# Filter taps sent through DRAM instead of turned on TensorE, in a gated mix of linear attention and a long convolution on one core

## The chip, the core and the metric

The kernel runs on one core of a Trainium2 chip. Its time is the device time of one execution in microseconds; the kernel before takes 174.07 us (median of three runs, 173.83 to 174.19). Engines are named as the profile names them: PE is TensorE's matmul and PEld its weight load, DVE is VectorE, ACT is ScalarE, POOL is GpSimd, SP is SyncE, whose queue issues nearly all transfers.

## The reference, cut to what matters

A sequence `x` of S = 2048 rows with D = 448 features goes through a linear attention block and through a state-space convolution, and a gate mixes the two:

```python
g = sigmoid((x * gate_w).sum(-1, keepdims=True))
qkv = x @ wqkv                                  # 16 heads of 28
pq, pk = phi(q), phi(k)                         # phi(t) = (t + 1 if t > 0 else exp(t)) + 1e-6
kv, z = sum over s of pk[s]^T v[s], sum over s of pk[s]
a = (pq @ kv / (pq . z + 1e-6)) @ wo
dt = exp(log_dt);  A = -exp(log_A_real) + 1j*A_imag;  C = (C_real + 1j*C_imag)*dt
K[d, l] = 2 * Re(sum over n of C[d, n] * exp(A[d, n]*dt[d]*l))      # N = 256
b = causal convolution of x with K along the sequence + x * D_skip
out = g*a + (1 - g)*b
```

With these inputs the exponent is so small that, channel by channel, `K[d, l]` is the same tap for all lags; the kernel tests this and has a general path behind a branch that isn't taken. So the convolution is a running sum of `x` times one tap per channel: 448 taps.

## The kernel before, in words

The sequence is cut into NC = 16 chunks of 128 rows. The matmuls split each fp32 operand into a high part and a low part, so that one projection of a chunk is 11 products. The order of all instructions is written out by hand; each engine works off its own queue in that order, and SP's queue too.

The main loop runs over c = 2 to 13 (L476). At step c PE computes the key projection of chunk c+1 (`project` with tag "k" or "v1", L484), the query projection of chunk c (L494), 11 products into the sums `g` (`do_g(c)`, L518), and from c = 5 on two running sums of two products each (`do_v`, L408). So one step is 37 products on PE. Around it:

- `split_t(c + 2)` casts the turned chunk on ACT (L240) and makes its low part `xt` on POOL (L241, shown as L236, the helper `low`). The second product of the next step's key projection reads that low part.
- `k_feature`, `k_high`, `k_low` (L357 to L372) work on the key projection in its PSUM bank "k"; the last instruction of `k_low` frees the bank for the next step's projection.
- `q_post` (L379) does the same for the query projection.
- `split_n(c + 2)` casts the plain chunk on ACT (L246), makes the low part `xn` on POOL, and with `skip` (L252) puts `x * D_skip` into `y` on POOL.
- `v_post(c)` (L413) multiplies the running sum of a chunk, in PSUM bank "v0" or "v1" by parity, with the taps `near` on DVE (L415), sends the last row to `u` with two small transfers on SP (L418), and adds the product to `y` on POOL (`v_add`, L423).
- `load_x(c + 3)` (L478) asks for a chunk of `x`, on SP, as the first thing of the step; there are four buffers.

The taps come from `s4d_prepare` (L279), a generator that `steps` advances a bit in each of the steps c = 1 to 5. Its small sums on DVE, on 112 partitions by 4 columns, end with `p0` in step 4 (L308). Channel d = 112 j + r stands at partition r, column j. In step 5, between the query projection and `do_g(5)`, its last part (L311 to L314) turns `p0`, spread over 128 columns, with four TensorE transposes into a PSUM bank, and ACT copies the bank to `near`, the first of the two parts of `rows`: every partition then holds all 448 taps in the order of the channels.

`VS` (L35) says which running sums belong to which step: 0 and 1 to step 5, 2 and 3 to step 6, and so on; the first of a pair stands behind the key projection, the second behind the query projection. Step 5 is an exception: its sum 1 stands behind `do_g(5)`, and `v_post(0)` and `v_post(1)` stand on either side of the instructions of `split_n(7)`.

The parameters of the sums come in as `abc`, four pieces of 112 x 1024 numbers, in the place of the chunks 6 to 15 of `pq` (L205, L229). The last chunk of `pq` is written only near the end, by `late`.

Of the kernel before, what the change touches and what calls it, by code (L numbers as in the profile page):

```python
# [7 lines left out]
F32 = mybir.dt.float32  # L8
# [3 lines left out]
ALU = mybir.AluOpType  # L12
# [3 lines left out]
P = 128  # L16
S = 2048
D = 448
# [3 lines left out]
NC = S // P  # L22
J = 4
DJ = D // J
# [7 lines left out]
QA = 1  # L32
QW = 512
EDGE = 16
VS = {c: (2 * c - 10, 2 * c - 9) for c in range(5, 11)} | {c: (c + 1,) for c in range(11, NC - 1)}  # L35
SMALL = 2.0 ** -70
FLAT = 2.0 ** 35
BIG = 3.4028234e38
# [102 lines left out]
def gated_mix_kernel(ctx: ExitStack, tc: tile.TileContext, xin, wq_d, wvo_d, abc_d, ldt_d, dsk_d,  # L141
                     turn_d, cst_d, first_d, gin_d, out):
    nc = tc.nc
    PE, ACT, DVE, POOL, SP = nc.tensor, nc.scalar, nc.vector, nc.gpsimd, nc.sync

    keep = ctx.enter_context(tc.tile_pool(name="keep", bufs=1))
    pq = keep.tile([P, NC, D], F32, name="pq")
# [9 lines left out]
    work = ExitStack()  # L157
# [7 lines left out]
    ident, trir = both[:, 0], both[:, 1]  # L165
# [5 lines left out]
    near, dsk = (rows[:, i * D:(i + 1) * D] for i in range(2))  # L171
# [12 lines left out]
    xn_p = work.enter_context(tc.tile_pool(name="xn", bufs=7))  # L184
    tp = work.enter_context(tc.tile_pool(name="tp", bufs=2))
    ps = work.enter_context(tc.tile_pool(name="ps", bufs=1, space=PSUM))

    warm = tp.tile([P, 512], mybir.dt.bfloat16, name="warm", tag="e")
    POOL.memset(warm, 1.0)
# [7 lines left out]
    def load_x(c):  # L197
        r = xp.tile([P, XC], F32, name="xr", tag="xr")
        turned[c], plain[c] = r[:, :NAT], r[:, NAT:]
        SP.dma_start(out=r, in_=xin[c])  # L200
# [4 lines left out]
    abc = pf[:DJ, 3 * J * N:7 * J * N].rearrange("p (i j n) -> p i j n", i=4, j=J)  # L205
    wkr = {}
    o = 0
    for part in PARTS:
# [8 lines left out]
        o = e  # L217
# [8 lines left out]
    SP.dma_start(out=dsk, in_=dsk_d.to_broadcast([P, D]))  # L226
    load_x(3)
    SP.dma_start(out=ldt, in_=ldt_d)
    for i in range(4):  # L229
        SP.dma_start(out=abc[:, i], in_=abc_d[:, i])  # L230
        if i == 0:
            load_x(4)
    SP.dma_start(out=both, in_=turn_d)

    def low(eng, o, r, h):
# [2 lines left out]
    def split_t(c):  # L238
        w = xt[c] = xt_p.tile([P, 2 * NAT], F32R, name="xt", tag="t")
        ACT.copy(w[:, :NAT], turned[c])  # L240
        low(POOL, w[:, NAT:], turned[c], w[:, :NAT])  # L241
# [33 lines left out]
    def small():  # L275
        cnt[0] += 1
        return sm[:, cnt[0] - 1]

    def s4d_prepare():  # L279
        tt = lambda eng, o, a, b, op: eng.tensor_tensor(out=o, in0=a, in1=b, op=op)  # L280
        stt = lambda o, a, k, b, op1: DVE.scalar_tensor_tensor(out=o, in0=a, scalar=k, in1=b, op0=ALU.mult, op1=op1)
        junk = [yf[:DJ, F0 + (i - 2) * 2 * N:F0 + (i - 1) * 2 * N].rearrange("p (i n) -> p i n", i=2) for i in range(2)]
        s0, s1, dt, am, p0, p1, d2, md, b0, b1 = (small() for _ in range(10))
        for j in range(J):
            ACT.activation(abc[:, 0, j], abc[:, 0, j], AF.Exp)
        ACT.activation(dt, ldt, AF.Exp)
        tt(DVE, d2, dt, dt, ALU.mult)
        yield
        for j in range(J):
            ACT.activation(junk[0], abc[:, 0:2, j], AF.Square, accum_out=am[:, j:j + 1])  # L290
            ACT.activation(junk[0][:, 0], abc[:, 2, j], AF.Copy, accum_out=s0[:, j:j + 1])
            DVE.scalar_tensor_tensor(out=junk[1], in0=abc[:, 2:4, j], scalar=1.0, in1=abc[:, 0:2, j], op0=ALU.mult,
                                     op1=ALU.mult, accum_out=s1[:, j:j + 1])
            if j % 2:
                yield
# [12 lines left out]
        tt(DVE, p0, p0, okc, ALU.mult)  # L308
        DVE.tensor_reduce(out=oks, in_=okc, op=ALU.add, axis=AX.X)
        yield  # L310
        o = ps.tile([P, 512], F32, name="p", tag="v1")  # L311
        for j in range(J):
            PE.transpose(o[:, j * DJ:(j + 1) * DJ], p0[:, j:j + 1].to_broadcast([DJ, P]), ident[:DJ, :DJ])
        ACT.copy(near, o[:, :D])  # L314

    def pieces(c, wh, wl, n, tag, last=None):
        o = ps.tile([P, 512], F32, name=tag, tag=tag)
# [20 lines left out]
    def project(*args, **kw):  # L338
        o, run = pieces(*args, **kw)
        run(11)  # L340
        return o
# [15 lines left out]
    def k_feature(c, o):  # L357
        e = tp.tile([P, D], F32, name="e", tag="e")
        pks[c] = o[:, :D]
        ACT.activation(e, pks[c], AF.Relu, scale=-1.0)  # L360
        ACT.activation(e, e, AF.Exp, scale=-1.0)  # L361
        DVE.scalar_tensor_tensor(out=pks[c], in0=pks[c], scalar=1.0, in1=e, op0=ALU.add, op1=ALU.max)  # L362

    def k_high(c):
        pkh[c] = tp.tile([P, 512], F32R, name="pkh", tag="pkh")[:, EDGE:EDGE + D]
        ACT.add(pkh[c], pks[c], 1e-6)

    def k_low(c):
        pk = pks.pop(c)
        pkl[c] = tp.tile([P, 512], F32R, name="pkl", tag="pkl")[:, EDGE:EDGE + D]  # L370
        for o, a, op in ((pkl[c], pkh[c].bitcast(F32), ALU.subtract), (zb, zb, ALU.add))[::-1 if c == NC - 1 else 1]:
            DVE.scalar_tensor_tensor(out=o, in0=pk, scalar=1e-6, in1=a, op0=ALU.add, op1=op)  # L372
# [33 lines left out]
    vt = {}  # L406

    def do_v(c):  # L408
        v = vt[c] = ps.tile([P, 512], F32, name="v", tag="v%d" % (c % 2))
        PE.matmul(v[:, :D], lhsT=tri, rhs=xn[c][:, :D], start=True, stop=False)  # L410
        PE.matmul(v[:, :D], lhsT=tri, rhs=xn[c][:, XC - NAT:], start=False, stop=True)

    def v_post(c):  # L413
        t = tp.tile([P, D], F32, name="t", tag="v0")
        DVE.tensor_tensor(out=t, in0=vt.pop(c)[:, :D], in1=near, op=ALU.mult)  # L415
        if c < NC - 1:
            for k in (c, UL + c):
                SP.dma_start(out=u[k:k + 1], in_=t[P - 1:P])  # L418
            v_add(c, t)
        return t  # L420

    def v_add(c, t):
        POOL.tensor_tensor(out=y[:, c], in0=y[:, c], in1=t, op=ALU.add)  # L423

    prep = s4d_prepare()
# [48 lines left out]
    split_n(3)  # L474
    woh, wol = [], []
    for c in range(2, NC - 2):  # L476
        if c + 3 < NC:
            load_x(c + 3)  # L478
        if c == 2:
            SP.dma_start(out=cst, in_=cst_d)  # L480
        if c == 4:
            SP.dma_start(out=wvo, in_=wvo_d)
        vs = VS.get(c, ())
        ko = project(c + 1, wkh, wkl, D, "v1" if c in (2, 4) else "k")  # L484
        for v in vs[:1]:
            do_v(v)
        split_t(c + 2)
        k_feature(c + 1, ko)
        k_high(c + 1)
        if c > 5:  # L490
            for v in vs[:1]:
                v_post(v)
        k_low(c + 1)
        qo = project(c, wqh, wql, D + 2, "q")  # L494
        if c == 5:
            steps(1)
        else:
            for v in vs[1:]:
                do_v(v)
        q_post(c, qo)  # L500
        if c == 10:
            split_n(c + 2)
        if c == 5:
            v_post(0)
        else:
            for v in vs[1:]:
                v_post(v)
        if c < 5:
            steps(2 if c == 4 else 1)
        if c == 3:  # L510
            DVE.tensor_copy(tri, trir)
            DVE.tensor_copy(gcr, gcat)
        if c == 7:
            SP.dma_start(out=okr[:, None, :DJ], in_=oks[:, None, :])
        if c == 9:
            DVE.tensor_reduce(out=okr[:, DJ:], in_=okr[:, :DJ], op=ALU.add, axis=AX.X)
            DVE.tensor_copy(okn, okr[:, DJ:])
        do_g(c)  # L518
        if c == 5:
            do_v(1)  # L520
        if c < 4:
            skip(c - 1)
        if c != 10:
            split_n(c + 2)
        if c == 5:
            v_post(1)
        for j in {11: (0, 1), 12: (2, 3)}.get(c, ()):
            w = xn_p.tile([P, NX], F32R, name="wo", tag="n")[:DJ, :2 * D].rearrange("p (i d) -> p i d", i=2)
            woh.append(w[:, 0])
            wol.append(w[:, 1])  # L530
            ACT.copy(woh[j], wo[:, j])
            low(POOL, wol[j], wo[:, j], woh[j])
# [109 lines left out]
    c = NC - 2  # L642
# [294 lines left out]
```

## Time and profile before

| | |
|---|---|
| time, median of 3 runs | 174.07 us (173.83 to 174.19) |
| the profiled execution | 174.06 us, its span 172.2 us |
| PE busy | 167.8 us in 876 products |
| PEld, DVE, ACT, POOL busy | 152.0, 113.9, 96.0, 120.0 us |
| granted TensorE clock | 1.00 throughout |
| moved by DMA | 18.60 MB, mean 108 GB/s |

A row of the timeline gives the start and the duration in us, the engine and line, the operation, what it writes and reads, the shape, how often it stands there in a row, and in brackets the idle time of the engine before it and what ended that. SPq rows are the issue of a transfer, not the transfer. A row of a group gives the count, the busy time in us, the mean in ns, and the idle time before. Times are from the span's start. The profile's line numbers are those of the kernel before.

### The profile page before, as it was taken

Reading aid. Unit: us, or ns where it says so; the run is one execution under the profiler, and the core shown is the slowest. Engines: PE = TensorE matmul, PEld = TensorE weight load, DVE = VectorE, ACT = ScalarE, POOL = GpSimd, SP = SyncE. Lnnn points to the kernel's source line nnn. Section 1 sums busy time; section 2 is a strip of 40 time slices with the busy share of each in tenths; the row PEclk is TensorE's granted clock in tenths of the full one; section 3 lists DMA queues with packets and bytes.
Section 4 is the critical chain, followed back from the end, with each engine's and each line's share of the span. In section 5 each row is a group of like instructions: output and inputs, shape, how many; then the busy total and the mean of one; then the engine's idle time right before and its main releaser. Section 6 shows DMA issues by size and latency. Waiting matters only on the chain. (4 is left out here: it accounts for less than half of the span.)

```text
span 172.2 us, 2796 instructions
## 1 busy us (share of the span) xinstructions
PE 167.8 (97%) x876; PEld 152.0 (88%) x876; DVE 113.9 (66%) x240; ACT 96.0 (56%) x221; POOL 120.0 (70%) x128
## 2 busy tenths in 40 slices
PE   6999999999999999999999999999999999999992
PEld 2788999999899999999999999999899999999992
DVE  0847737698975483846627346487898998987542
ACT  3688588894256262542727456356574564664541
POOL 6082667877529988696996999529968998892200
PEclk9999999999999999999999999999999999999999
DMA  5989975097003031230404200000031222122213
GB/s 173 415 297 294 268 209 166 0 368 303 4 0 114 11 123 34 95 123 1 122 15 131 106 1 1 0 0 2 7 67 54 107 89 76 62 99 107 108 59 108
DMA packets 7962, 18.60 MB, mean 108 GB/s; under 512 B 2045, under 2 KB 4810, under 8 KB 7818
## 3 DMA queue, kind: packets, MB, share of 16 engines
q1 hardware_dynamic: 7802, 18.30, 32.0%
q8 instruction: 7, 0.11, 0.3%
q10 hardware_dynamic: 144, 0.11, 0.2%
q14 instruction: 9, 0.07, 0.1%
HBM read 14.38 MB, written 3.67 MB: 105 GB/s over the span
## 5 line engine op out<-in xcount | busy, mean ns | idle before, releaser
L629 PE MATMUL a<-wk,th 128*128 128x448 f32 (+1 forms) x170 | 36.4, 360 | 0.0
L403 PE MATMUL g<-pkh,xn 128*128 128x448 f32 x112 | 35.6, 364 | 0.0
L629 PEld LDWEIGHTS a<-wk,th 128*128 128x128 f32 x170 | 29.5, 189 | 1.6
L334 PE MATMUL k<-wk,xt 128*128 128x448 f32 x132 | 29.3, 367 | 0.0
L334 PE MATMUL q<-wqh,xt 128*128 128x450 f32 x120 | 27.5, 366 | 0.0
L362 DVE SCALAR_TENSOR_TENSOR k<-k,e 128x448 f32<-128x448 f32 x12 | 7.6, 632 | 29.4 <-ACT e L361 29.4
L423 POOL TENSOR_TENSOR y<-y,t 128x448 f32<-128x448 f32 x16 | 18.7, 1168 | 11.5 <-DVE t L415 11.5
L334 PEld LDWEIGHTS k<-wk,xt 128*128 128x128 f32 x132 | 24.8, 189 | 2.2 <-DVE wk L236 0.3
L334 PEld LDWEIGHTS q<-wqh,xt 128*128 128x128 f32 x120 | 22.5, 188 | 1.7
L236 POOL TENSOR_TENSOR xn<-xr,xn 128x448 fp32r<-128x448 f32 x16 | 19.4, 1211 | 6.6 <-ACT xn L246 4.5
L403 PE MATMUL g<-pkl,xn 128*128 128x448 f32 x64 | 23.4, 366 | 0.0
L403 PEld LDWEIGHTS g<-pkh,xn 128*128 128x128 f32 x112 | 21.0, 188 | 2.2
L236 POOL TENSOR_TENSOR xt<-xr,xt 128x512 fp32r<-128x512 f32 x14 | 18.2, 1297 | 5.9 <-ACT xt L240 5.9
L360 ACT ACTIVATE e<-k 128x448 f32<-128x448 f32 x12 | 6.5, 544 | 26.9 <-PE k L334 26.9
L542 POOL TENSOR_TENSOR prod<-pq,zb 128x448 f32<-128x448 f32 x16 | 18.6, 1172 | 4.1 <-ACT zb L665 3.0
L252 POOL TENSOR_TENSOR y<-xr,rows 128x448 f32<-128x448 f32 x16 | 18.8, 1175 | 0.0
L567 POOL TENSOR_TENSOR pn<-pq,den 128x336 f32<-128x336 f32 x16 | 12.3, 771 | 5.9 <-ACT den L556 4.1
L634 DVE SCALAR_TENSOR_TENSOR ot<-y,og,a 128x448 f32<-128x448 f32 (+1 forms) x17 | 10.7, 629 | 5.1 <-PE a L629 5.1
L612 DVE TENSOR_TENSOR th<-tr,th 128x512 fp32r<-128x512 f32 x16 | 11.0, 691 | 2.7 <-ACT th L611 2.1
L403 PEld LDWEIGHTS g<-pkl,xn 128*128 128x128 f32 x64 | 11.2, 174 | 1.2 <-DVE pkl L372 0.2
L611 ACT CAST th<-tr 128x512 fp32r<-128x512 f32 x16 | 9.4, 588 | 4.6 <-PE tr L604 4.4
L334 PE MATMUL q<-wql,xt 128*128 128x450 f32 x45 | 11.6, 364 | 0.0
(150 smaller groups left out, 302.3 us busy)
## 6 DMA issues: line engine op xcount, KB each, us to landing
xr<-in SPq DMA_DIRECT2D x15, 512.0 KB, 6.2
out<-ot SPq DMA_DIRECT2D x15, 224.0 KB, 1.9
pq<-in SPq DMA_DIRECT2D x4, 448.0 KB
wvo<-in SPq DMA_DIRECT2D x1, 1792.0 KB
y<-in SPq DMA_DIRECT2D x2, 480.0 KB
y<-in SPq DMA_DIRECT2D x2, 450.0 KB
u<-t SPq DMA_DIRECT2D x30, 1.8 KB, 1.7
y<-in SPq DMA_DIRECT2D x1, 448.0 KB, 4.3
```

Of the source, the lines that this page charges most:

```text
L236: eng.tensor_tensor(out=o, in0=r, in1=h.bitcast(F32), op=ALU.subtract)
L252: POOL.tensor_tensor(out=y[:, c], in0=plain[c][:, :D], in1=dsk, op=ALU.mult)
L334: PE.matmul(o[:, :n], lhsT=a, rhs=b, start=run.n == 1, stop=not seq)
L362: DVE.scalar_tensor_tensor(out=pks[c], in0=pks[c], scalar=1.0, in1=e, op0=ALU.add, op1=ALU.max)
L403: PE.matmul(g[i][:a.shape[1], :D], lhsT=a, rhs=b, start=c == 0 and n == 0, stop=c == NC - 1 and n == len(seq) - 1)
L423: POOL.tensor_tensor(out=y[:, c], in0=y[:, c], in1=t, op=ALU.add)
L542: POOL.tensor_tensor(out=pd[c], in0=pq[:, c], in1=zb, op=ALU.mult)
L567: POOL.tensor_tensor(out=n[:, :3, :DJ].rearrange("p j (h d) -> p j h d", h=4), in0=a, in1=r[:, :H - 4].rearrange("p (j h) -> p j h", j=3)[ ...
L611: ACT.copy(h, ov)
L612: DVE.tensor_tensor(out=l, in0=ov, in1=h.bitcast(F32), op=ALU.subtract)
L629: PE.matmul(a[:, lo:hi], lhsT=u_, rhs=w_[:, lo:hi], start=n == 0, stop=n == 10)
L634: DVE.scalar_tensor_tensor(out=ot[:, lo:hi], in0=y[:, c, lo:hi], scalar=og[:, c:c + 1], in1=a[:, lo:hi], op0=ALU.mult, op1=ALU.add)
```

## The change

- The four transposes and ACT's copy out of PSUM go. In their place SP sends `p0` to a DRAM row `nd` in 112 pieces of 16 bytes (four columns of a partition), and then reads the row back into all 128 partitions of the last chunk of `pq`, which is free by then. The row is in the order (r, j), so the taps stand there with a stride of four numbers.
- The first products read this place with a stride: `v_post` of chunks 0 and 1 in step 5, both behind `split_n(7)`, and of chunks 2 and 3, both behind the query projection of step 6. ACT then copies the taps into `near`, in channel order, at the end of step 6.
- The two transfers stand on SP at the start of step 5, behind the requests for two chunks of `x`; from there on each step asks for chunk c + 4 instead of c + 3.
- `abc` comes in two transfers instead of four, with the request for chunk 4 between them.

```diff
-VS = {c: (2 * c - 10, 2 * c - 9) for c in range(5, 11)} | {c: (c + 1,) for c in range(11, NC - 1)}
+VS = {c: ((2 * c - 10,), (2 * c - 9,)) for c in range(5, 11)} | {c: ((c + 1,), ()) for c in range(11, NC - 1)}
+VS[5], VS[6] = ((0,), ()), ((), (2, 3))
...
+    nd = work.enter_context(tc.tile_pool(name="nd", bufs=1, space=bass.MemoryType.DRAM)).tile([1, D], F32, name="nd")
...
-    for i in range(4):
-        SP.dma_start(out=abc[:, i], in_=abc_d[:, i])
-        if i == 0:
-            load_x(4)
+    SP.dma_start(out=abc[:, :2], in_=abc_d[:, :2])
+    load_x(4)
+    SP.dma_start(out=abc[:, 2:], in_=abc_d[:, 2:])
...
-        yield
-        o = ps.tile([P, 512], F32, name="p", tag="v1")
-        for j in range(J):
-            PE.transpose(o[:, j * DJ:(j + 1) * DJ], p0[:, j:j + 1].to_broadcast([DJ, P]), ident[:DJ, :DJ])
-        ACT.copy(near, o[:, :D])
...
+    taps = pq[:, NC - 1].rearrange("p (r j) -> p j r", j=J)
+
-    def v_post(c):
+    def v_post(c, w=None):
+        w = near.rearrange("p (j r) -> p j r", j=J) if w is None else w
         t = tp.tile([P, D], F32, name="t", tag="v0")
-        DVE.tensor_tensor(out=t, in0=vt.pop(c)[:, :D], in1=near, op=ALU.mult)
+        DVE.tensor_tensor(out=t.rearrange("p (j r) -> p j r", j=J),
+                          in0=vt.pop(c)[:, :D].rearrange("p (j r) -> p j r", j=J), in1=w, op=ALU.mult)
...
     for c in range(2, NC - 2):
-        if c + 3 < NC:
-            load_x(c + 3)
+        for i in (c + 3,) if c < 5 else (c + 3, c + 4) if c == 5 else (c + 4,):
+            if i < NC:
+                load_x(i)
...
+        if c == 5:
+            SP.dma_start(out=nd.rearrange("o (r j) -> (o r) j", j=J), in_=p0)
+            SP.dma_start(out=pq[:, NC - 1], in_=nd.to_broadcast([P, D]))
...
         qo = project(c, wqh, wql, D + 2, "q")
-        if c == 5:
-            steps(1)
-        else:
-            for v in vs[1:]:
-                do_v(v)
+        for v in vs[1]:
+            do_v(v)
         q_post(c, qo)
...
         if c == 5:
-            v_post(1)
+            v_post(0, taps)
+            v_post(1, taps)
+        if c == 6:
+            ACT.copy(near.rearrange("p (j r) -> p j r", j=J), taps)
```

On PE the only instructions that go are the transposes, between the query projection of chunk 5 and the sums of step 5 (`q` and `g` are PSUM banks; the same rows stand there with the rest in place). Before:

```order
L410 MATMUL v<-xn,tri 128x448
L411 MATMUL v<-xn,tri 128x448
L334 MATMUL q<-wqh,xt 128x450 x8
L334 MATMUL q<-wql,xt 128x450 x3
L313 MATMUL p<-both,sm 128x112 x4
L403 MATMUL g_142<-pkh,xn 128x448
```

In the changed kernel the row of L313 isn't there, and in step 6 the two rows of `do_v(2)` move from ahead of the query projection to behind it.

On POOL, from the low part `xt` of chunk 7 in step 5 to that of chunk 9 in step 7 (`xn` and `y<-xr` are `split_n` and its `skip`, `y<-y,t` is `v_add`). Before:

```order
L236 TENSOR_TENSOR xt<-xr,xt 128x512
L423 TENSOR_TENSOR y<-y,t 128x448
L236 TENSOR_TENSOR xn<-xr,xn 128x448
L252 TENSOR_TENSOR y<-xr,rows 128x448
L423 TENSOR_TENSOR y<-y,t 128x448
L236 TENSOR_TENSOR xt<-xr,xt 128x512
L423 TENSOR_TENSOR y<-y,t 128x448 x2
L236 TENSOR_TENSOR xn<-xr,xn 128x448
L252 TENSOR_TENSOR y<-xr,rows 128x448
L236 TENSOR_TENSOR xt<-xr,xt 128x512
```

The same stretch in the changed kernel:

```order
L237 TENSOR_TENSOR xt<-xr,xt 128x512
L237 TENSOR_TENSOR xn<-xr,xn 128x448
L253 TENSOR_TENSOR y<-xr,rows 128x448
L423 TENSOR_TENSOR y<-y,t 128x448 x2
L237 TENSOR_TENSOR xt<-xr,xt 128x512
L423 TENSOR_TENSOR y<-y,t 128x448 x2
L237 TENSOR_TENSOR xn<-xr,xn 128x448
L253 TENSOR_TENSOR y<-xr,rows 128x448
L237 TENSOR_TENSOR xt<-xr,xt 128x512
```

The work of `split_n(7)` has moved ahead of the first add, and both adds of chunks 0 and 1 now stand ahead of the low part of chunk 8; the adds of chunks 2 and 3 stay behind it.

More of the change, by code (lines that the diff above doesn't have):

```diff
@@ L282, in s4d_prepare @@
         junk = [yf[:DJ, F0 + (i - 2) * 2 * N:F0 + (i - 1) * 2 * N].rearrange("p (i n) -> p i n", i=2) for i in range(2)]
-        s0, s1, dt, am, p0, p1, d2, md, b0, b1 = (small() for _ in range(10))
+        s0, s1, dt, am, p1, d2, md, b0, b1 = (small() for _ in range(9))
         for j in range(J):
@@ L423, in v_add @@
         POOL.tensor_tensor(out=y[:, c], in0=y[:, c], in1=t, op=ALU.add)
+    p0 = small()
     prep = s4d_prepare()
@@ L482, in gated_mix_kernel @@
             SP.dma_start(out=wvo, in_=wvo_d)
-        vs = VS.get(c, ())
+        if c == 5:
+            SP.dma_start(out=nd.rearrange("o (r j) -> (o r) j", j=J), in_=p0)
+            SP.dma_start(out=pq[:, NC - 1], in_=nd.to_broadcast([P, D]))
+        vs = VS.get(c, ((), ()))
         ko = project(c + 1, wkh, wkl, D, "v1" if c in (2, 4) else "k")
-        for v in vs[:1]:
+        for v in vs[0]:
             do_v(v)
@@ L490, in gated_mix_kernel @@
         if c > 5:
-            for v in vs[:1]:
+            for v in vs[0]:
                 v_post(v)
@@ L502, in gated_mix_kernel @@
             split_n(c + 2)
[L503 to L507, printed above, removed]
+        for v in vs[1]:
+            v_post(v, taps if c == 6 else None)
         if c < 5:
```

## The prediction

> **What bounds the kernel now.** I read the page's busy line first, then the list of who waits for whom, for the weight loads, then the timeline around the instructions that the change touches, and last the transfers.
>
> ```profile
> PE 167.8 (97%) x876; PEld 152.0 (88%) x876; DVE 113.9 (66%) x240; ACT 96.0 (56%) x221; POOL 120.0 (70%) x128
> ```
> ```profile
> PEld p L313 <- DVE sm L280: 0.2, 1, 0.2
> ```
> ```profile
> 41.60:49.50 7.90, 7.90 (x42) 7.15 (x42) 7.00 (x21) 4.12 (x10) 3.67 (x3) 1.00 0.07 26
> ```
>
> PE is busy for 97% of the span, and once the main loop runs, hardly anything holds it: the list of the weight loads has no longer wait there than this one of 0.2 us, at the transposes that go. In the stretch from 41.6 to 49.5 us, where the change sits, it is busy for all 7.90 us, at a clock of 1.00. So PE's queue sets the time. An edit gains what it takes off PE, and costs what it makes PE wait; the other engines matter only by how late they hand PE something.
>
> **What comes off PE.** The timeline at the end of the query projection of step 5:
>
> ```profile
> 45.84 0.59 PEld L334 LDWEIGHTS q<-wql,xt 128*128 128x128 f32 x3
> ...
> 46.44 0.16 DVE L280 TENSOR_TENSOR sm<-sm,okc 112x4 f32<-112x4 f32 x1
> ...
> 46.66 0.38 PEld L313 LDWEIGHTS p<-both,sm 112*128 112x128 f32 x4 [0.23 <-DVE sm L280]
> ...
> 47.00 0.19 PEld L403 LDWEIGHTS g<-pkh,xn 128*128 128x128 f32 x1
> ```
>
> The last weight load of the projection ends at 45.84 + 0.59 = 46.43; the first one of the sums begins at 47.00. Between them lie a wait of 0.23 us for `p0` (DVE's L280, done at 46.44 + 0.16 = 46.60) and the four transposes. With these gone the sums begin at 46.43: 0.57 us come off.
>
> **How much of it PE can use at once.** Next PE needs bank "k" for the key projection of step 6. These rows carry that and the later bounds:
>
> ```profile
> 48.36 0.61 DVE L372 SCALAR_TENSOR_TENSOR zb<-k,zb 128x448 f32<-128x448 f32 x1
> ...
> 49.38 0.62 DVE L353 SCALAR_TENSOR_TENSOR pq<-q,t 128x448 f32<-128x448 f32 x1
> ...
> 49.53 2.21 PEld L334 LDWEIGHTS k<-wk,xt 128*128 128x128 f32 x11
> ...
> 50.68 1.16 POOL L423 TENSOR_TENSOR y<-y,t 128x448 f32<-128x448 f32 x1 [5.11 <-DVE t L415]
> ...
> 54.37 0.19 PEld L410 LDWEIGHTS v<-xn,tri 128*128 128x128 f32 x1
> ...
> 55.13 1.30 POOL L236 TENSOR_TENSOR xt<-xr,xt 128x512 fp32r<-128x512 f32 x1
> ...
> 56.98 2.19 PEld L334 LDWEIGHTS k<-wk,xt 128*128 128x128 f32 x11
> ...
> 61.34 1.29 POOL L236 TENSOR_TENSOR xt<-xr,xt 128x512 fp32r<-128x512 f32 x1
> ...
> 64.41 1.59 PEld L334 LDWEIGHTS k<-wk,xt 128*128 128x128 f32 x8
> ```
>
> DVE frees bank "k" at 48.36 + 0.61 = 48.97. That time doesn't move with PE: DVE works its small sums off without a break up to `p0` and goes straight on. PE would be there at 49.53 − 0.57 = 48.96; the hand-over took 0.06 us for `p0` (46.60 to 46.66), so it starts at 49.03. A wait of 0.07 us takes the place of the one removed, and 0.50 us is left. Between 0.50 and 0.57 I take 0.50. From here on I count PE's own times 0.50 us earlier.
>
> **When the taps arrive.** Two transfers in a row take the place of ACT's copy. No row shows a small write to DRAM read back, so I bound each half by its neighbours:
>
> ```profile
> xr<-in SPq DMA_DIRECT2D x15, 512.0 KB, 6.2
> out<-ot SPq DMA_DIRECT2D x15, 224.0 KB, 1.9
> ...
> u<-t SPq DMA_DIRECT2D x30, 1.8 KB, 1.7
> ```
> ```profile
> DMA to landing us min/median/max: 3.6/6.2/10.9
> ```
>
> SP can issue the first at 46.65: it has nothing ahead but requests for `x` whose buffers were free long before, and the DMA engines are at rest (share 0.07 in the stretch of 41.6 to 49.5). The first moves 1.8 KB, as `u<-t` does (1.7 us), into DRAM, as `out<-ot` does (1.9 us): I take 1.9. SP then waits for it and issues the second, 224 KB out of DRAM: between 1.9 us (`out<-ot`, same size, other direction) and 3.6 us (the quickest `xr<-in`, more than twice the size); I take 2.7, about the middle. The taps are there at T = 46.65 + 1.9 + 2.7 = 51.25 (bounds 46.65 + 1.7 + 1.9 = 50.25 and 46.65 + 1.9 + 3.6 = 52.15). DVE, free at 49.38 + 0.62 = 50.00, waits there for about 1.2 us.
>
> **Who waits for that.** With a product of s on DVE (0.615 us each before, first row of the next block), the first is done at T + s, the second at T + 2s.
> - Banks "v0" and "v1": `do_v(2)` and `do_v(3)` now stand together behind the query projection of step 6. The second begins at 54.37 − 0.50 = 53.87, the first two products (0.20 each, 2.21 for 11) earlier, at 53.47. They need T + s below 53.4 and T + 2s below 53.8: T up to 52.6.
> - Bank "k": `k_feature(7)` stands behind the two products. From it to the end of `k_low` DVE and ACT take some 2.4 us, and PE comes at 56.48: T + 2s + 2.4 below 56.4, T up to 52.8.
> - POOL: behind the first product come two adds (some 1.17 each, the 1.16 above and like it) and the low part of chunk 8 (1.30). Its reader is the second product of the key projection, at 56.98 + 0.20 − 0.50 = 56.68: T + 0.615 + 0.05 + 2.34 + 1.30 below 56.68, T up to 52.4. Before, POOL stood still here for 5.11 us; `split_n(7)` now goes into that idle time, so it isn't in this chain.
> - POOL later: the product of chunk 2 now falls where that of chunk 3 was, so one add more lies between there and the low part of chunk 9. That is then done by 61.34 + 1.29 − 0.50 + 1.17 = 63.30, read at 64.41 + 0.20 − 0.50 = 64.11. That holds, with 0.8 to spare.
>
> The tightest limit, 52.4, is 1.15 us behind my T and 0.25 behind its late bound. So the two transfers and the wait on DVE cost nothing.
>
> **The strided products.** Four products on DVE and one copy on ACT read one number in four. The nearest rows:
>
> ```profile
> L415 DVE TENSOR_TENSOR t<-v,rows 128x448 f32<-128x448 f32 x16 | 9.8, 615 | 0.0
> ...
> L570 DVE TENSOR_TENSOR pn<-pq,den 128x48 f32<-128x48 f32 x16 | 3.1, 195 | 0.0
> ...
> L734 DVE TENSOR_TENSOR k<-k,cst 112x112 f32<-112x112 f32 x1 | 0.3, 273 | 0.0
> ```
>
> A plain product is 273 ns for 112 numbers and 615 for 448: 1.02 ns a number and 159 fixed. That makes 208 ns for 48; L570, which reads twelve separate runs of four, took 195. So jumping cost nothing there, and I take s = 0.615. But L570's runs hold four numbers and here each is alone, so I keep s up to three times that, 1.85 us, for the range. At s = 0.615 none of it shows, and ACT's copy (0.53 us before) stands in step 6 where ACT idles. The Trainium skill, page "SBUF — State Buffer", section on Door 1, says that SBUF has lines of 16 bytes and that an access that goes to a new line pays a penalty; a stride of four fp32 does so at every number. It gives no price; L570 starts a line for every four and shows none.
>
> **`abc` and `x`.** Chunk 4 now stands behind 448 KB more. It was asked for at 8.35:
>
> ```profile
> 8.35 0.35 SPq L200 DMA_DIRECT2D xr<-in  x1
> ```
> ```profile
> 24.43 0.62 ACT L240 CAST xt<-xr 128x512 fp32r<-128x512 f32 x1
> ```
>
> Even with the longest landing of any `xr`, 10.9 us, it was there at 19.25; 448 KB more, at half the landing of an `xr` of 512 KB under load (6.2), makes some 22.4, ahead of the cast at 24.43. Two issues fewer on SP cost PE nothing. The earlier requests for `x` move nothing on PE either: it waits for no `xr` in the list.
>
> **The sum.** The profiled execution took 174.06 us, as good as the median (174.07): 174.06 − 0.57 + 0.07 = 173.56. What comes after step 6 is ordered as before and follows PE.
>
> **The rivals.**
> 1. *The strided products are slow, and the kernel gets slower.* The place is DVE in step 5, behind the taps. At T = 51.25, `do_v(3)` waits once 2s passes 53.8 − 51.25 = 2.55, so s = 1.28, twice the row; the gain is gone at s = 1.53. At s = 1.85 the second product ends at 54.95, PE waits 1.15, and the time is 174.06 − 0.50 + 1.15 = 174.7. For it: no row reads numbers one by one. Against it: L570. Chance 0.11. The skill's rule of lines, above, works in this direction.
> 2. *The taps come late.* Past T = 52.4 PE waits by what T is late, and from 52.9 on the kernel is slower. One more small trip of 1.9 us gives T = 53.15, a wait of 0.75, and 174.3; a second transfer at the median `xr`, 6.2, gives T = 54.75 and 175.9. For it: 112 pieces of 16 bytes into DRAM are in no row. Against it: the engines rest. Chance 0.09. The Trainium skill, "DMA: Bandwidth & Descriptors", section "Specifications", has it that below 512 bytes the engines read, modify and write; `u<-t`, far below that, landed in 1.7 us, though not in DRAM.
> 3. *The gain is lost at a hand-over.* Step 6 begins only when bank "k" is free, and a little more there (an ACT cast or a POOL step in DVE's way) leaves 0.1 to 0.3 us of the gain: 173.8 to 174.0. For it: the slack of the bank is nil. Against it: DVE's chain to 48.97 has no other engine's new work in it. Chance 0.14.
>
> **How the numbers follow.** My forecast has 0.66 and its own range is 173.35 to 173.75. A measurement of this kernel can tell about 0.2%, 0.35 us, from no change; the forecast's 0.50 is not far past it, so I put 0.07 of the 0.66 within. Faster: 0.59. Within: 0.07 + 0.14 from the third rival + 0.01 from the edge of the second = 0.22. Slower: 0.11 + 0.08 = 0.19. The low end is 0.57 off and a run's spread (174.07 − 173.83 = 0.24): 173.3. The high end takes in the third rival and the start of the second, 174.2; the far ends of the first two, 174.7 to 175.9, are the part left out.
>
> **What would show it.** Right: the weight loads go from L334 straight to the sums `g`; a wait of under 0.1 us for DVE's `zb` at the start of step 6; the two transfers issued at about 46.65 and 48.6; DVE idle until about 51.3, waiting for a DMA; products of about 0.62; POOL's low part of chunk 8 done by 55.6. Wrong: a wait of PE in step 6 or 7 for a product (`v` banks) or for POOL's `xt`, products over 1.2 us, or the first transfer landing after 50.

## The result: slower by 0.34%, and the profile after

The changed kernel takes 174.61 us (median of 19 runs, 174.14 to 176.76), the kernel before on the same chip 173.98 (173.57 to 174.55). The ratio is 1.0034, with a 95% interval of 1.0022 to 1.0045; the one run of 176.76, in a slower state, is not in it. Forecast was 173.56. The profiled execution took 174.84 us, its span 173.1.

The page's busy line of the kernel after, and from the list of who waits for whom the two rows of the weight loads that are new (waiting engine and line, what it waits for: us in total, times, the longest):

```profile
PE 168.1 (97%) x872; PEld 151.7 (88%) x872; DVE 116.6 (67%) x240; ACT 96.2 (56%) x221; POOL 120.1 (69%) x128
```
```profile
PEld k L330 <- POOL xt L237: 0.4, 1, 0.4
PEld q L330 <- issue: 0.4, 1, 0.4
```

The wait for `p0` is gone and PE has four instructions fewer; two waits of 0.4 us that before did not have stand in their place. The timeline of after shows where. First step 4's end and step 5:

```profile
42.19 1.38 DVE L346 TENSOR_SCALAR t<-e 128x448 f32<-128x448 f32 x1
44.09 0.62 DVE L349 SCALAR_TENSOR_TENSOR pq<-q,t 128x448 f32<-128x448 f32 x1 [0.51 <-DVE t L346]
...
44.83 1.54 PEld L330 LDWEIGHTS q<-wqh,xt 128*128 128x128 f32 x8 [0.36 <-issue]
...
46.38 0.59 PEld L330 LDWEIGHTS q<-wql,xt 128*128 128x128 f32 x3
...
46.98 0.19 PEld L399 LDWEIGHTS g<-pkh,xn 128*128 128x128 f32 x1
47.02 0.33 SPq L486 DMA_DIRECT2D nd<-sm  x1
...
48.42 0.33 SPq L487 DMA_DIRECT2D pq<-nd  x1
...
49.59 2.20 PEld L330 LDWEIGHTS k<-wk,xt 128*128 128x128 f32 x11
...
52.60 1.83 DVE L414 TENSOR_TENSOR t<-v,pq 128x448 f32<-128x448 f32 x2 [1.21 <-DMA pq<-nd]
```

The same two DVE instructions in the timeline of before:

```profile
41.93 1.38 DVE L350 TENSOR_SCALAR t<-e 128x448 f32<-128x448 f32 x1
43.42 0.62 DVE L353 SCALAR_TENSOR_TENSOR pq<-q,t 128x448 f32<-128x448 f32 x1
```

The transposes' gap is closed: the sums `g` start right behind the query projection (46.38 + 0.59 = 46.97, 46.98). But the query projection itself begins late. It needs bank "q", which the product of `q_post(4)` frees. That product starts 0.51 us behind the end of its operand (43.57 to 44.09) where before it took 0.11 (43.31 to 43.42). Nothing that the profile names ended this wait: the operand was there, and in the trace the waiting instruction ahead of the product is over at 43.63, 0.45 us before it starts. I call such a standstill of an engine, with nothing left to wait for, a stop.

Then steps 6 to 8 of after, DVE, POOL and PEld, each ahead of who reads it (the first PEld row is `do_v(3)`):

```profile
58.12 1.81 DVE L414 TENSOR_TENSOR t<-v,pq 128x448 f32<-128x448 f32 x2
```
```profile
55.92 1.30 POOL L237 TENSOR_TENSOR xt<-xr,xt 128x512 fp32r<-128x512 f32 x1
59.14 2.27 POOL L423 TENSOR_TENSOR y<-y,t 128x448 f32<-128x448 f32 x2 [1.92 <-DVE t L414]
...
63.60 1.44 POOL L237 TENSOR_TENSOR xt<-xr,xt 128x512 fp32r<-128x512 f32 x1
```
```profile
54.48 0.19 PEld L406 LDWEIGHTS v<-xn,tri 128*128 128x128 f32 x1
...
64.52 0.19 PEld L330 LDWEIGHTS k<-wk,xt 128*128 128x128 f32 x1
65.09 1.91 PEld L330 LDWEIGHTS k<-wk,xt 128*128 128x128 f32 x10 [0.38 <-POOL xt L237]
```

The low part of chunk 9 is done at 63.60 + 1.44 = 65.04; the second product of the key projection of step 8 wanted it at 64.71 (64.52 + 0.19). The first product behind `q_post(6)` stands in the timeline of before at:

```profile
57.33 0.61 DVE L415 TENSOR_TENSOR t<-v,rows 128x448 f32<-128x448 f32 x1
```

And the last weight load of the program, before and after:

```profile
168.72 0.19 PEld L629 LDWEIGHTS a<-rc,th 112*128 112x128 f32 x1
```
```profile
169.09 0.19 PEld L631 LDWEIGHTS a<-rc,th 112*128 112x128 f32 x1
```

The page gives the span to one place (172.2, 173.1); in the trace the last record ends at 172.23 and 173.06. From the end of the last weight load to there, "the end" from here on, it is 3.32 us before and 3.78 after, though the change touches nothing behind it. In that stretch the timeline has rows for the last product, copies and a transfer only; the trace keeps the waiting instructions too. SP first waits for the transfers and then drains (DRAIN, the record behind its last wait for one). With their times on the profile's scale these records read:

```
SP at the end            last wait for a transfer    drain            span
before                   record 159 at 171.34        160 at 171.40    172.23
after                    record 161 at 171.70        162 at 172.12    173.06
(records of SP counted from 0, waiting instructions included; each wait takes 0.03 us)
```

In after SP stands still for 0.39 us between its last wait and the drain, with nothing to wait for, and the drain takes 0.12 instead of 0.01. Before, too, SP stands for 0.42 us ahead of its record 162, but there that falls into a wait behind the drain: from the drain to the end of the span it takes 0.83 us, as in the kernels below whose record 162 is a wait for a transfer.

Measured from weight load to weight load the difference comes out nearly whole. Each step runs from the first load of one key projection to the next one's; the start is the time to the first such load of step 5 (41.62 and 41.88).

| us | before | after | difference |
|---|---|---|---|
| start, up to step 5 | 41.62 | 41.88 | +0.26 |
| step 5 | 7.91 | 7.71 | −0.20: transposes −0.44, bank "q" +0.24 (split by the runs below) |
| step 6 | 7.45 | 7.50 | +0.05 |
| step 8 | 7.43 | 7.72 | +0.29: POOL's `xt` |
| the end: last weight load to end of span | 3.32 | 3.78 | +0.46: SP |

All other steps agree within 0.02. The start's difference is there in the projections of the first chunks already (9.44 against 9.70 us), and the start varies: it lies between 41.41 and 41.83 in the five kernels of this document with `abc` in four transfers, and between 41.19 and 42.20 in those with two, so I count it as chance. Without it the table makes −0.20 + 0.05 + 0.29 + 0.46 = +0.60, and the medians differ by 0.63.

### The profile page after: what moved, and what is told of

It is laid out like the page before. It is cut to its first block, busy times and chain, and to the rows that moved or that the text cites. A ratio compares the mean times of both kernels' runs of the same rounds, so it can differ in the third digit from the quotient of the medians.

```text
span 173.1 us, 2791 instructions
## 1 busy us (share of the span) xinstructions
PE 168.1 (97%) x872; PEld 151.7 (88%) x872; DVE 116.6 (67%) x240; ACT 96.2 (56%) x221; POOL 120.1 (69%) x128
## 5 line engine op out<-in xcount | busy, mean ns | idle before, releaser
L330 PE MATMUL k<-wk,xt 128*128 128x448 f32 x132 | 29.8, 369 | 0.0
L346 DVE TENSOR_SCALAR t<-e 128x448 f32<-128x448 f32 x15 | 11.6, 775 | 1.9 <-ACT e L345 1.9
```

Source lines behind the costliest of these rows:

```text
L330: PE.matmul(o[:, :n], lhsT=a, rhs=b, start=run.n == 1, stop=not seq)
L346: DVE.tensor_scalar(out=t, in0=e, scalar1=1.0, scalar2=1e-6, op0=ALU.min, op1=ALU.add)
```

## Experiments

Each kernel was compared with before on its own chip; a ratio is to before. "Step 5", "step 8" and "end" are as in the table.

**After, once more** (no edit).

> The changed kernel once more, for a second profile of it. What my account of its first profile calls caused by the change should stand there again: a wait of PE of about 0.38 us for the low part of chunk 9 in step 8, products with a stride of about 0.95 us, the second transfer landing about 4.1 us after its issue, and no transposes. What it calls chance should differ: the 0.26 us that PE was later than before at the start of the loop, and the 0.5 us that the span ended later after the last product. Open is the wait of 0.36 us of PE without a releaser at 44.5 us, at the start of the query projection of step 5: if the earlier request for chunk 9 causes it, it is there again within 0.1 us; if it is chance it is not. Time about 1.003 of before.

174.59 us, ratio 1.0031 (1.0014 to 1.0047). Step 5 is 7.69, the end 3.78: as in the first execution. Step 8 is 7.49: POOL's `xt` is only just late here, because the taps landed 0.3 us sooner. So step 5 and the end lose the same each time, and step 8 loses what the transfer leaves.

**The request for chunk 9 behind the taps' transfers.**

```diff
-        for i in (c + 3,) if c < 5 else (c + 3, c + 4) if c == 5 else (c + 4,):
+        for i in (c + 3,) if c <= 5 else (c + 4,):
...
             SP.dma_start(out=pq[:, NC - 1], in_=nd.to_broadcast([P, D]))
+            load_x(9)
```

> The changed kernel with the request for chunk 9 put behind the two transfers of the taps, so that the DMA engines rest at 42.8 us as before. Theory (the 0.36 us wait of PE without a releaser at 44.5 us is an instruction fetch held up by the transfer of chunk 9): the wait is gone and PE is 0.28 us earlier from there on, time about 174.3. Rival (the wait comes from the place in the code, or is chance): it stays or comes and goes as in the repeat, time about 174.6. In both the wait of 0.38 us in step 8 stays, unless the later chunk 9 makes it longer.

Ratio 1.0073 (1.0045 to 1.0100). The wait at the query projection stays, at 0.37, so the request for `x` is not its cause. In this position the 512 KB run beside the taps, which come later (4.7 us from the issue of the second transfer to DVE's start, instead of 4.2); DVE's row and what PE waits for:

```profile
52.45 1.81 DVE L414 TENSOR_TENSOR t<-v,pq 128x448 f32<-128x448 f32 x2 [1.74 <-DMA pq<-nd]
```
```profile
PEld v L406 <- DVE t L414: 0.6, 1, 0.6
PEld k L330 <- POOL xt L237: 0.5, 1, 0.5
```

PE's start was 0.7 us earlier in this execution and the taps were no earlier, so they were late for it: the limit on the `v` banks was real, with a wait of 0.56 us there.

**The adds of chunks 2 and 3 behind the low part of chunk 9.**

```diff
-            v_add(c, t)
+            if c in (2, 3):
+                late_adds.append((c, t))
+            else:
+                v_add(c, t)
...
         split_t(c + 2)
+        if c == 7:
+            for a in late_adds:
+                v_add(*a)
```

> The changed kernel with the adds of chunks 2 and 3 on POOL put behind the low part of chunk 9 instead of ahead of it; everything else is the same. Theory (PE's wait in step 8 is the length of POOL's chain from the late, slow products through two adds to that low part): the 0.38 us wait is gone, time 0.3 to 0.4 us below the changed kernel, about 174.25. Rival (the gain was lost elsewhere, and POOL has another late hand-over one step on): the wait moves to step 9, time unchanged at 174.6.

174.41 us, ratio 1.0021 (1.0003 to 1.0039). Step 8 is back at 7.44; step 5 (7.67) and the end (3.79) stay. The time is 0.2 us under the repeat where 0.3 to 0.4 was expected, and the intervals of the two ratios overlap: that the wait is gone is shown by the trace, not by the time.

**Taps in channel order in DRAM**, so that nothing is read with a stride: 448 pieces of 4 bytes.

```diff
-            SP.dma_start(out=nd.rearrange("o (r j) -> (o r) j", j=J), in_=p0)
+            SP.dma_start(out=nd.rearrange("o (j r) -> (o r) j", j=J), in_=p0)
...
-    taps = pq[:, NC - 1].rearrange("p (r j) -> p j r", j=J)
+    taps = pq[:, NC - 1].rearrange("p (j r) -> p j r", j=J)
```

> The changed kernel with the row in DRAM written in channel order, in 448 pieces of 4 bytes, so that the products and ACT's copy read without a stride. Theory (the stride costs a third of a us a product, and that is what pushes POOL's chain over in step 8): the four products take 0.62 instead of 0.95, the copy 0.53 instead of 1.03, the low part of chunk 9 is ready 0.6 us earlier and PE's wait in step 8 is gone, 0.3 to 0.4 us below the changed kernel. Rival (the late landing alone does it): the products get shorter but the wait stays at 0.1 us or more. If four times as many pieces make the first transfer land later than 1.4 us after its issue, the wait on DVE grows by as much and the time with it.

181.44 us, ratio 1.0433 (1.0401 to 1.0465). The products take 617 ns, the copy 582. The rows of the groups of after, the second and the third with the stride:

```profile
L414 DVE TENSOR_TENSOR t<-v,rows 128x448 f32<-128x448 f32 x12 | 7.4, 614 | 0.0
L414 DVE TENSOR_TENSOR t<-v,pq 128x448 f32<-128x448 f32 x4 | 3.6, 949 | 1.2 <-DMA pq<-nd 1.2
...
L528 ACT COPY rows<-pq 128x448 f32<-128x448 f32 x1 | 1.0, 1034 | 0.0
```

So the stride costs 0.33 us a product and 0.45 us in the copy. But the first transfer grew; SP's rows of this kernel, and PE's wait:

```profile
47.06 0.35 SPq L486 DMA_DIRECT2D nd<-sm  x1
53.28 0.33 SPq L487 DMA_DIRECT2D pq<-nd  x1
```
```profile
PEld v L406 <- DVE t L414: 4.1, 1, 4.1
```

SP issued the second transfer 6.2 us behind the first, in after 1.4 us. In the trace all 448 pieces are through at 48.35, and the landing is told between 51.5 and 53.3, so it isn't the pieces' own time. With pieces of 4 bytes the change costs 4.3%.

**`abc` in two transfers, and nothing else of the change** (before with that one edit).

```diff
-    for i in range(4):
-        SP.dma_start(out=abc[:, i], in_=abc_d[:, i])
-        if i == 0:
-            load_x(4)
+    SP.dma_start(out=abc[:, :2], in_=abc_d[:, :2])
+    load_x(4)
+    SP.dma_start(out=abc[:, 2:], in_=abc_d[:, 2:])
```

> Before, with abc in two transfers instead of four and nothing else changed. Theory 'place in the queue': the product of query step 4 on DVE starts some 0.5 us behind its operand, PE waits 0.36 us at the query projection of step 5, and the kernel is 0.28 us slower than before, about 174.3 (ratio 1.0016). Rival 'the taps' part of the change': no such wait, ratio 1.000, since transposes, transfers and products are those of before.

174.53 us, ratio 1.0025 (1.0012 to 1.0038). Its list of waits has the row of after:

```profile
PEld q L333 <- issue: 0.4, 1, 0.4
```

Step 5 is 8.10, 0.19 over before (the transposes are still in, and `p0` makes PE wait 0.12 instead of 0.23, since PE is late itself). The end is 3.44, 0.12 over before. The part of the change that I had put at nothing makes the kernel slower by itself.

**After, with one small instruction more at the start of DVE's queue.**

```diff
     POOL.memset(u, 0.0)
+    DVE.memset(sm[:, 15], 0.0)
```

> After, with one more small instruction on DVE at the very start, where DVE idles 4 us (a memset of 112x4 numbers nobody reads). Theory 'place in the queue': DVE stands still for 0.45 us ahead of one certain instruction, counted from the start of its queue; after has one waiting instruction fewer on DVE than before (abc in two transfers instead of four), which put that stop in front of the product of query step 4 (L382). One instruction more moves it off: the row DVE pq<-t loses its idle 0.5 us, PE's idle 0.36 at the query projection of step 5 goes, about 0.28 us of time is won: 0.9984 of after, about 174.3. Rival 'something of the transfers': the idle time stays at 0.36 and the time is that of after, 174.6.

174.33 us, ratio 1.0007 (0.9993 to 1.0022). Step 5 is 7.46. The two DVE rows stand 0.11 apart again, as before:

```profile
41.51 1.38 DVE L347 TENSOR_SCALAR t<-e 128x448 f32<-128x448 f32 x1
43.00 0.62 DVE L350 SCALAR_TENSOR_TENSOR pq<-q,t 128x448 f32<-128x448 f32 x1
```

An instruction that nobody reads, 40 us earlier, takes the wait away. In the 8 traces with 327 records on DVE (waiting instructions counted) the 64th record is this product, and DVE is idle for 0.45 us ahead of it; in the 9 with 328 the 64th record is the waiting instruction ahead of the product, and no idle time shows.

**The same with the adds late.** Edits as in the two kernels above.

> After, with the small instruction on DVE at the start and with the two adds of chunks 2 and 3 on POOL behind the low part of chunk 9. If the losses are the stop on DVE (0.28) and POOL's late xt in step 8 (0.29 at most), and the transposes are worth 0.48, both waits are gone and about 0.45 us is won on before: 173.6 (ratio 0.9975). Rival 'the rest is elsewhere' (in the start or the tail, where after took 0.2 to 0.5 us more in its profile): ratio 0.9995 to 1.001, 174.0 to 174.2.

174.04 us, ratio 1.0004 (0.9991 to 1.0017). Steps 5 and 8 are 7.47 and 7.44: both waits of PE are gone, and still the kernel is only level with before. The end is 3.78. So the rest of the loss is there.

**Before without the transposes and the copy.** The taps are left out: `near` is filled with ones.

```diff
-        yield
-        o = ps.tile([P, 512], F32, name="p", tag="v1")
-        for j in range(J):
-            PE.transpose(o[:, j * DJ:(j + 1) * DJ], p0[:, j:j + 1].to_broadcast([DJ, P]), ident[:DJ, :DJ])
-        ACT.copy(near, o[:, :D])
...
     POOL.memset(u, 0.0)
+    POOL.memset(near, 1.0)
```

> Before without the four transposes and the copy of the taps: near is filled with ones by POOL at the start, so the taps are left out; all else is that of before. My theory of the prediction: PE's queue gives all of it back but a wait on bank k, 0.50 us, 173.5 (ratio 0.9971). What after's trace says: 0.48 us (173.55, ratio 0.9972), the first weight load of the sums right behind the query projection. Rival 'lost at a hand-over later': below 0.2 us, ratio above 0.9989.

173.91 us, ratio 0.9987 (0.9973 to 1.0001); its profiled execution took 173.49, 0.57 under that of before. The weight loads:

```profile
45.83 0.59 PEld L330 LDWEIGHTS q<-wql,xt 128*128 128x128 f32 x3
46.43 0.19 PEld L399 LDWEIGHTS g<-pkh,xn 128*128 128x128 f32 x1
...
49.07 0.56 PEld L330 LDWEIGHTS k<-wk,xt 128*128 128x128 f32 x3
```

The sums start at 46.43 and the next key projection at 49.07, where I had put 46.43 and 49.03. Step 5 is 7.47, 0.44 shorter; the rest agrees with before. That is what the transposes are worth by the trace; the ratio's middle says 0.23, its interval reaches 0.47. So the times bear out neither the 0.50 of the forecast nor the 0.48, and don't exclude that part of it is lost later; what speaks for 0.44 is the trace.

**Two small transfers more on SP in before**, into a spare tile.

```diff
+        if c == 8:
+            for i in range(2):
+                SP.dma_start(out=edge[:DJ, i * J:(i + 1) * J], in_=ldt_d)
```

> Before, with two transfers more on SP in step 8: 112x4 numbers each into a spare tile that nobody reads. Theory 'place in the queue' for SP: SP too stands still for about 0.4 us ahead of a certain instruction of its queue (the record 162 of SP), and in after that is the drain at the very end, which the end of the program waits for; in before it is two records later, in a wait that lasts anyway. Two instructions more put it on the drain: from the last weight load of PE to the end of the span 3.8 us instead of 3.3, the rows of PE unchanged, and the kernel about 0.5 us slower than before: ratio 1.003, 174.5. Rival 'transfers of after at the end' or no such place: ratio 1.000.

174.86 us, ratio 1.0054 (1.0036 to 1.0072). PE's steps are those of before, the end is 4.22. The drain is now record 162 of SP, and SP stands still for 0.40 us in front of it, as forecast. But 0.4 us more comes from elsewhere: SP's last waits go through the eight semaphores of the transfers in a fixed order, 0.07 us each. Counted in the traces, before and after have 96 transfers, this kernel 98, the one with `abc` alone 94 (the 114 of an expectation below stands in no trace). With 96 the two transfers that land last are at the end of that list, with 98 they are at its head, and the list is worked off behind them. With 94 two waits are left behind the last one, which makes the 0.12 at the end of the kernel with `abc` alone.

**After with `abc` in four transfers**, and **the same with the adds late.**

```diff
-    SP.dma_start(out=abc[:, :2], in_=abc_d[:, :2])
-    load_x(4)
-    SP.dma_start(out=abc[:, 2:], in_=abc_d[:, 2:])
+    for i in range(4):
+        SP.dma_start(out=abc[:, i], in_=abc_d[:, i])
+        if i == 0:
+            load_x(4)
```

> After, with abc in four transfers as before: one waiting instruction more on DVE, two more instructions on SP. Theory 'place in the queue' says that both stops go, DVE's in step 4 (PE's idle 0.36 us in step 5) and SP's at the end (0.5 us); what is left is the transposes' 0.48 less 0.05 in step 6 and 0.05 to 0.3 for POOL's late xt in step 8: 173.75 (ratio 0.9977 to 0.9993, 0.9985 the middle), 0.8 us under after. Rival 'stops stay, elsewhere': ratio 1.002 or more.

> After, with abc in four transfers as before and the adds of chunks 2 and 3 behind the low part of chunk 9 on POOL. All four losses found so far are out: 174.05 - 0.48 + 0.05 = 173.6 (ratio 0.9975), the fastest of all. If the stops come back at another place, 1.000 or more.

Ratios 1.0033 (1.0018 to 1.0048) and 1.0017 (1.0002 to 1.0032): my expectation of the end was wrong. Step 5 is 7.47 and 7.48, so DVE's part held. But these have 98 transfers, and the end is 4.10 in both: the list of waits comes last, and SP's stop, still at record 162, falls into it. The expectation had not counted the order of the semaphores.

**Both stops off, with 96 transfers as in after.** One number per partition is set to zero at the start, where the second transfer of `abc` writes later. That makes one instruction more on DVE and, because the transfer now has to wait for DVE as well as for a semaphore, one waiting instruction more on SP.

```diff
     POOL.memset(u, 0.0)
+    DVE.memset(pq[:, NC - 1, :1], 0.0)
```

> After, with a memset of one number per partition on DVE at the start, in the place that abc's second transfer fills later. That is one instruction more on DVE, and on SP one waiting instruction more (the second transfer of abc now waits for DVE too), with the same 114 transfers. Theory 'places in the queues': DVE's stop leaves the product of query step 4 (0.28 us) and SP's stop moves off the drain into the wait ahead of it, so that the end shortens from 3.8 to 3.3 us: 0.8 us under after, ratio to before 0.9977 to 0.9995 (the transposes' 0.48 less 0.05 in step 6 and up to 0.3 for POOL's late xt). Rival: the end of after is long for another reason; then this is as the kernel with the pad alone, 1.0007.

173.86 us against 174.20, ratio 0.9976 (0.9963 to 0.9990). The last weight load, with the span at 172.01:

```profile
168.48 0.19 PEld L632 LDWEIGHTS a<-rc,th 112*128 112x128 f32 x1
```

The end is 3.34. Record 162 of SP is now the last wait for a transfer, which lasts anyway, and the drain follows it after 0.06 us. Step 5 is 7.46, step 8 7.60.

**The same with the adds late.**

> The same with the adds of chunks 2 and 3 behind the low part of chunk 9 on POOL. If the stop on DVE, the stop on SP and POOL's late xt are all that took the gain, 174.05 - 0.48 + 0.05 = 173.6, ratio 0.9975, faster than both kernels. If something is still missing, 0.999 or more.

173.86 us, ratio 0.9983 (0.9969 to 0.9997). No wait over 0.07 us is left in steps 5 to 8 (7.48, 7.46, 7.43, 7.43); the weight loads of step 8 run on:

```profile
63.90 2.19 PEld L331 LDWEIGHTS k<-wk,xt 128*128 128x128 f32 x11
```

The end is 3.35. The intervals of these two kernels overlap: what the late adds give beyond the other edit isn't measured, but both are faster than before and than after.

**SP's stop alone off.** The same number is set by POOL, so that DVE's queue stays as in after.

```diff
     POOL.memset(u, 0.0)
+    POOL.memset(pq[:, NC - 1, :1], 0.0)
```

> After, with the memset of one number per partition on POOL instead: SP gets its waiting instruction more, DVE is as in after. Theory: the end is 0.5 us shorter (3.3 instead of 3.8 us behind the last weight load), PE's idle 0.36 us in step 5 stays: 174.1, ratio to before 0.9995 to 1.001, against after's 1.0034. Rival: the end stays at 3.8 and the ratio at 1.003.

173.79 us, ratio 0.9989 (0.9973 to 1.0004), where after has 1.0034. The end is 3.34, PE's 0.36 at the query projection stays (step 5: 7.70). The stop on SP is shown by itself.

**The second transfer from 128 different rows.** It reads chunk 0 of `x` instead of the taps' one row; the taps are left out.

```diff
-            SP.dma_start(out=pq[:, NC - 1], in_=nd.to_broadcast([P, D]))
+            SP.dma_start(out=pq[:, NC - 1], in_=xin[0][:, NAT:LO])
```

> After, with the second transfer reading the 128 rows of chunk 0 of x (1792 bytes each, at different addresses) instead of 128 times the one row of the taps; the taps are left out. Theory 'one row read 128 times is slow' (packets of 0.26 us mean, 1.08 the longest, 4 us from issue to landing): packets near those of the output, 0.07 us mean, and landing within about 2.5 us of the issue, so DVE does not wait for it. Rival 'the way out of DRAM costs that': packets of 0.2 us and more, landing 4 us after its issue.

It need not wait for the first transfer, so only the time from its issue is to be compared, in one execution. SP's and DVE's rows:

```profile
46.79 0.43 SPq L487 DMA_DIRECT2D pq<-in  x1
...
50.16 0.62 DVE L349 SCALAR_TENSOR_TENSOR pq<-q,t 128x448 f32<-128x448 f32 x1
50.71 0.94 DVE L414 TENSOR_TENSOR t<-v,pq 128x448 f32<-128x448 f32 x1
```

DVE doesn't wait for it. In the trace the 128 packets of 1792 bytes take 0.085 us on average and are through 2.3 us behind the issue; in the two executions of after, where all read one row, 0.26 and 0.20 us, and 3.9 and 3.4 us. Reading one row 128 times costs 1.1 to 1.6 us here, as far as this one pair of kernels tells: the row of the taps has also just been written, and the rows of `x` have not.

## Why the prediction was wrong, step by step

- **"Two issues fewer on SP cost PE nothing" was the step that failed.** The prediction put this at nothing and gave no reason. I looked at what the transfers deliver and when, and not at what their number does to the queues of DVE and SP. Fewer transfers mean one wait fewer on DVE, and that put a stop of 0.45 us in front of the product that frees bank "q" (+0.24 on PE). On SP `abc` and the taps together left the number of transfers at 96, but brought two waiting instructions more, and that put a stop in front of the drain (+0.46). No view of before has a row for either. Together, 0.70 us, they are more than the gain of 0.50 that was forecast; taken out, the kernel is faster by 0.24% (0.10% to 0.37%), on the forecast's side.
- **The transposes** were put at 0.57, 0.50 of it usable. The step without them is 0.44 shorter by the trace (0.23, up to 0.47, by the times). The next key projection began at 49.07 where 49.03 was forecast; the mechanism held.
- **The taps' landing** was put at T = 51.25, 52.15 at the latest; DVE started at 52.60. The first transfer took 1.4 us (1.9 forecast), the second 4.15 (2.7, 3.6 at most). The bounds came from transfers that read different rows. That the `v` banks, bank "k" and the low part of chunk 8 cost no wait was partly luck: the second product ended at 52.60 + 1.83 = 54.43, and `do_v(3)` began at 54.48; the low part was done at 57.22 and wanted at 57.28. PE itself began step 6 at 49.59, 0.56 us later than forecast; in the run with chunk 9 behind the taps, where PE was earlier, it waited at the `v` bank.
- **The strided products** were put at s = 0.615 and took 0.949; ACT's copy took 1.03 us, and 0.58 without the stride. That is below the 1.28 from which the first rival begins, and no wait of PE for a product shows. L570 was the wrong neighbour, and was misread: it reads four runs of twelve numbers and writes twelve runs of four, so it hardly jumps where it reads. The Trainium skill, "SBUF — State Buffer", section on Door 1, has a penalty for each access to a new line of 16 bytes; by that rule runs of twelve numbers pay once in four and single numbers each time, and the trace agrees (0.617 without the stride, 0.949 with it).
- **"POOL later"** had a spare of 0.8 us: done at 63.30, read at 64.11. It was done at 65.04 and wanted at 64.71. The order of POOL was counted rightly, but its idle time ahead was not: both adds wait for the first product behind `q_post(6)`, which starts at 58.12 instead of the 56.83 that the forecast implies (57.33 − 0.50), because DVE waited for the taps until 52.60 (in the run that reads 128 rows DVE begins at 50.71, and this product 1.89 us earlier too). That is 1.29; with 0.33 for the stride and 0.15 for a longer `xt` it makes 1.77, where 1.74 are to be explained. In the six executions that kept this order on POOL and the transfers of after, step 8 lost 0.06 to 0.29.
- **The rivals.** The slow stride (1) and the late taps (2) had their mechanisms, below the point from which each decides; together they made POOL late. The lost hand-over (3) came nearest, as it leaves 0.1 to 0.3 us of the gain, and step 5 gained 0.20: but the loss was at bank "q", not "k", and not through ACT or POOL. No rival had the end of the program.
- For the first transfer the Trainium skill, "DMA: Bandwidth & Descriptors", section "Specifications", has one rule for all pieces below 512 bytes (read, modify, write). The runs tell such pieces apart: 112 pieces of 16 bytes let the next transfer go 1.4 us later, 448 pieces of 4 bytes 6.2 us later.

## What to carry to other kernels

When an edit changes how many instructions or transfers an engine has, compare traces for a wait whose releaser was long done, and measure the time from the last weight load to the end of the span by itself: a few tenths of a microsecond there can have the sign of the whole result. Before giving up a change worth under 0.5%, shift the queues by one harmless instruction and measure again; here that turned 1.0034 into 0.9976. When work is put behind a new transfer, carry the transfer's late bound through every later chain, idle times included, not only to the first reader.

## What the runs showed of the hardware

- DVE and SP each stand still for 0.39 to 0.46 us at one fixed place of their queue, DVE in front of its 64th and SP in front of its 163rd record (waiting instructions counted), as far as it can be seen. On SP it showed ahead of the drain, of the next drain behind it (with the request for chunk 9 moved) and of a wait that had nothing to wait for (with 98 transfers). On DVE it showed ahead of one product only; that it lies under the 1.38 us instruction when it falls one record sooner is argued, not shown. What the stop is was not settled. The loading of instructions is a candidate that no run here tests. The transfers' view of after lists such transfers:

```profile
q8 instruction: 7, 0.11, 0.3%
q14 instruction: 10, 0.08, 0.2%
```

- One of these, of 8192 bytes on q14, keeps to DVE's place in the traces: it begins 0.66 to 0.95 us behind the start of the 64th record in the eight kernels with the stop, and 1.26 to 1.49 us ahead of it in the nine without. So it moves with the stop; but where there is one, it begins behind it, and that it has to do with the cause is not shown.
- At the end SP waits for the eight semaphores of the transfers one after the other, 0.07 us each. Which of them the last transfer uses depends on the number of transfers: with 96 of them the span ends 3.32 to 3.35 us behind the last weight load (3.77 to 3.79 with SP's stop ahead of a drain), with 94 it is 3.44, with 98 it is 4.10 to 4.22 with the stop in it.
- 128 packets of 1792 bytes from one row of DRAM took 0.20 to 0.26 us each, from 128 rows 0.085. Reading one fp32 in four cost DVE 0.33 us more on 448 columns, and ACT 0.45.
